# Linear attention's second pass: products of the features with the sums in row halves of the array, two heads each

## The chip, the cores and the metric

The kernel runs on one core of a Trainium2 chip. The metric is the device time of one execution in microseconds. Of the kernel before there are three runs (1293.9, 1294.66 and 1296.31 us; median 1294.66) and one profiled execution. Engines are named as in the profile: PE is the matmul engine (PEld its weight loads), DVE, ACT and POOL are the vector, scalar and general engines, SP issues the DMAs.

## The reference

Four layers are applied to x of 2048 tokens by 512, each as x + layer(layernorm(x)): A, B, A, B. The change lies in the A layers, linear attention with 32 heads of 16 columns:

```python
pq = jnp.einsum("bhsd,hdf->bhsf", q, w_phi)
pk = jnp.einsum("bhsd,hdf->bhsf", k, w_phi)
phi_q = jnp.concatenate([_softmax(pq, axis=-1), _softmax(-pq, axis=-1)], axis=-1)
phi_k = jnp.concatenate([_softmax(pk, axis=-1), _softmax(-pk, axis=-1)], axis=-1)
kv = jnp.einsum("bhsf,bhsd->bhfd", phi_k, v)
z  = jnp.einsum("bhsf->bhf", phi_k)
num = jnp.einsum("bhqf,bhfd->bhqd", phi_q, kv)
den = jnp.einsum("bhqf,bhf->bhq", phi_q, z)[..., None] + 1e-6
o = num / den
return (lambda x, *d: x.transpose(*d))(o, 0, 2, 1, 3).reshape(B, S, D) @ wo
```

A head has 32 features (two softmaxes of 16), so 4 heads fill 128 partitions. The B layers are causal softmax attention within four segments plus a memory over the segments before.

## The kernel before, in words

An A layer runs in two passes over 16 tiles of 128 tokens. `pass1` projects q, k and v, forms the features of k, and sums kv and z over all tokens into `kva`: 128 partitions (4 heads of 32 features), 8 groups g of 4 heads, 17 columns (16 of v and the ones column for z). At its end (L948 to L954) it builds `KN`, a block-diagonal copy of the sums: for each group 128 partitions by 4 heads x 17 = 68 columns, zero where the partition's head is not the column's. DVE does this with a 0/1 table (`bdA`, columns of the constant `bd`), four groups to an instruction.

`pass2` (L1017) then takes the tiles i = 0 to 15 one after the other. For each:

- `transposed` (L973) turns the features of q by PE into `f`, 128 features by 8 groups by 128 tokens. The transposes go in the two row halves of the array (64 tokens each, `tp_halves`, L183), into the banks mx and my (or lg), and ACT copies each half of the tokens to `f` (names P in the profile).
- `products` (L996) multiplies `f` with `KN`. For each group there are two matmuls in the two column halves of the array: 128 features by 64 tokens as weights, the 68 columns of `KN` moving, so that tokens 0 to 63 and 64 to 127 of four heads come out side by side in one bank. Features and sums are plain float32, and the trace records each matmul of that type twice (two passes, each with its own weight load). Most other matmuls are of a rounded type and recorded once.
- `weigh` (L551) divides by the ones column: a reciprocal and a multiplication on DVE, into the tile's output `o` (names U, later ot).
- `turn_halves` and `out_proj` turn `o` and multiply it with the output weight `wo` (names w; oh and ol are the halves of the turned tile). These matmuls fill all 128 rows and 128 columns.

PE's order is fixed: `held` (L165) ties every matmul to the one recorded before it. DVE, ACT, POOL and SP are held to their recorded order as well (`Ordered`, L145). PSUM has eight banks: four in rotation under the tag g, two under lg (taken together), mx and my.

For tiles 0 to 12 (`wide`) the products use both banks of lg, groups 0 to 3 in the first and 4 to 7 in the second, and one `weigh` takes both. The last three tiles run as side work in the opening of the B layer that follows (`steps`, L1494), between its first matmuls; lg is needed there, so each half of the groups takes one bank of g, and `weigh` takes it at once. `steps` hands out that side work over 11 slots by an estimate of PE time that `mm` (L174) adds up. The maxima of the B layer (`maxima`, L1256; CUSTOM_DVE_ANT_0 in the profile, ISA in the order of instructions) use banks mx, my and pairs of g in the same stretch.

In the profile all matmuls stand under L177, the transposes under L181 and L187, all operations of the other engines under L155.

Of the kernel before, what the change touches and what calls it, by code (L numbers as in the profile page):

```python
# [7 lines left out]
F32 = mybir.dt.float32  # L8
# [7 lines left out]
D = 512  # L16
H = 32
DH = 16
P = 128
# [3 lines left out]
VW = DH + 1  # L23
# [9 lines left out]
G = 4  # L33
# [68 lines left out]
def interleave_kernel(ctx, tc, x_in, a_wqkv, a_wphi, a_wo, b_wq, b_wk, b_wv, b_wo, b_beta,  # L102
                      c_ident, c_mask, c_bd, out):
    nc = tc.nc
    MUL, ADD, SUB, MAX, MIN = ALU.mult, ALU.add, ALU.subtract, ALU.max, ALU.min

    cp = ctx.enter_context(tc.tile_pool(name="cp", bufs=1))
    wp = ctx.enter_context(tc.tile_pool(name="wp", bufs=4))
    hp_ = ctx.enter_context(tc.tile_pool(name="hp", bufs=2))
    sp = ctx.enter_context(tc.tile_pool(name="sp", bufs=2))  # L110
# [5 lines left out]
    def nm(s):  # L116
        uid[0] += 1
        return f"{s}_{uid[0]}"
# [4 lines left out]
    def PS(tag, bufs, shape=(P, 512)):  # L123
        return ps.tile(list(shape), F32, tag=tag, bufs=bufs, name=nm(tag))
# [38 lines left out]
    dve, act, pool, sync = [Ordered(e) for e in (nc.vector, nc.scalar, nc.gpsimd, nc.sync)]  # L163
# [10 lines left out]
    def mm(*a, **k):  # L174
        n = a[0].free_size()
        work[0] += n / 2.26 if k["rhs"].dtype == F32R else (n * 2 / 2.4 + 25 if "tile_position" in k else 2 * max(112, n * 2 / 2.4))
        return held(nc.tensor.matmul(*a, **k))  # L177
# [13 lines left out]
        sync.dma_start(out=out.bitcast(F32), in_=in_.bitcast(F32))  # L191

    ident = cp.tile([P, P], F32, name="ident")
    bd = cp.tile([P, 27], F32, name="bd")
    bdA, bdB = bd[:, 0:8], bd[:, 8:16]
    mask = cp.tile([P, 512], F32, name="mask")
    gates = cp.tile([P, 2, H], F32, name="gates")
    eb = cp.tile([P, H], F32, name="eb")
# [3 lines left out]
    def constants():  # L202

        sync.dma_start(out=mask, in_=c_mask)
        sync.dma_start(out=eb, in_=b_beta.unsqueeze(0).broadcast_to([P, H]))
        yield
        yield
        act.activation(eb, eb, AF.Exp, scale=-1.0)
        dve.tensor_scalar(eb, eb, 1.0, None, op0=ADD)
        dve.reciprocal(gates[:, 1, :], eb)  # L210
        dve.tensor_scalar(gates[:, 0, :], gates[:, 1, :], -1.0, 1.0, op0=MUL, op1=ADD)
        for j in range(4):
            dve.tensor_copy(share[32 * j : 32 * j + 32, :].rearrange("p (c f) -> p c f", f=2),
                            gates[32 * j : 32 * j + 32, 0, :].rearrange("p (c j f) -> p j c f", j=4, f=2)[:, j])
        dve.tensor_scalar(share, share, -1.0, bd[:, 24:25], op0=ADD, op1=MUL)
        dve.tensor_scalar(share, share, 1.0, None, op0=ADD)
        dve.tensor_tensor(out=gates[:, 1, :].rearrange("p (c h) -> p c h", c=NC), op=MUL,
                          in0=gates[:, 1, :].rearrange("p (c h) -> p c h", c=NC),
                          in1=bdB.unsqueeze(1).broadcast_to([P, NC, 8]))
        dve.tensor_copy(ones, bd[0:32, 25:26].broadcast_to([32, P]))  # L220


    def wtiles(tag):
# [451 lines left out]
    class LayerA:  # L675
# [4 lines left out]
        def first(self, hT, vv, upcoming):  # L680
# [18 lines left out]

            for c in range(NC):  # L700
                pool.tensor_tensor(out=phibd[:, c], in0=wph[:, c, :].unsqueeze(1).broadcast_to([P, 8, DH]),
                                        in1=bd[:, 16:24].unsqueeze(2).broadcast_to([P, 8, DH]), op=MUL)
            kf, qf = [], []
            kfold, qfold = folded(kraw, kf), folded(qraw, qf)
            for t in range(4):
# [40 lines left out]
        def pass1(self, first):  # L746
# [44 lines left out]
            for n, s in enumerate(SEGS):  # L791
# [53 lines left out]
                if n < NSEG - 1:  # L845
                    hTs, g = upc
# [98 lines left out]
                self.e = {4 * s + i: e[4 + i] for i in range(3)}  # L945
                yield from self.transposed(0)
                yield from sums[1]
                KN = self.KN = sp.tile([P, 8, 4, VW], F32, tag="KN", bufs=1, name=nm("KN"))  # L948
                den = kva[:, :, DH]
                dve.tensor_scalar(den, den, 0.5e-6, None, op0=ADD)  # L950
                for g in (0, 4):
                    dve.tensor_tensor(out=KN[:, g : g + 4], op=MUL,
                                      in0=kva[:, g : g + 4, :].unsqueeze(2).broadcast_to([P, 4, 4, VW]),
                                      in1=bdA[:, 0:4].unsqueeze(1).unsqueeze(3).broadcast_to([P, 4, 4, VW]))  # L954
                exp(e[6])
                for j, _ in enumerate(qproj(3, e, later)):
                    if j == 1:
# [38 lines left out]
        def products(self, i):  # L996

            f, o = self.phT.pop(i), self.o
            wide = i <= NT - 4
            pns = PS("lg", 1, (P, 2, 512)) if wide else None  # L1000
            for half in range(2):
                pn = pns[:, half] if wide else PS("g", G)
                for q in range(4):
                    g = 4 * half + q
                    for a in (0, 64):
                        mm(pn[a : a + 64, q * 4 * VW : (q + 1) * 4 * VW], lhsT=f[:, g, a : a + 64],
                           rhs=self.KN[:, g].rearrange("p h e -> p (h e)"), start=True, stop=True,
                           tile_position=(0, a))
                if not wide:
                    weigh(o[:, half * 256 : half * 256 + 256].rearrange("p (g h d) -> p g h d", g=4, h=4),  # L1010
                          pn[:, 0 : 16 * VW].rearrange("p (g h e) -> p g h e", g=4, h=4), 0.0, False)
                elif half == 1:
                    weigh(o.rearrange("p (s h d) -> p s h d", s=2, h=16),
                          pns[:, :, 0 : 16 * VW].rearrange("p s (h e) -> p s h e", e=VW), 0.0, False)
                yield

        def pass2(self):  # L1017
# [686 lines left out]
```

## Time and profile before

| | |
|---|---|
| median of three runs | 1294.66 us |
| profiled execution | 1295.97 us, its span 1294.2 us |
| busy PE, PEld, DVE, ACT, POOL | 1257.7, 975.4, 1070.7, 838.5, 754.0 us |
| granted PE clock | 1.0 |
| KN built, first and second A layer | 171.8 and 803.4 us |
| first and last product of all | 173.3 and 904.5 us |

Busy shares are means over the whole span. Matmuls are pipelined: a matmul's row shows its full length from first weight to last result, so that neighbours overlap, and what one costs is read from the distance between starts. "128*64 128x68" in a row means weights of 128 rows by 64 columns and a moving part of 128 rows by 68 columns.

### The profile page before, as it was taken

Reading aid. Unit: us, or ns where it says so; the run is one execution under the profiler, and the core shown is the slowest. Engines: PE = TensorE matmul, PEld = TensorE weight load, DVE = VectorE, ACT = ScalarE, POOL = GpSimd, SP = SyncE. Lnnn points to the kernel's source line nnn. Section 1 sums busy time; section 2 is a strip of 40 time slices with the busy share of each in tenths; the row PEclk is TensorE's granted clock in tenths of the full one; section 3 lists DMA queues with packets and bytes.
Section 4 is the critical chain, followed back from the end, with each engine's and each line's share of the span. In section 5 each row is a group of like instructions: output and inputs, shape, how many; then the busy total and the mean of one; then the engine's idle time right before and its main releaser. Section 6 shows DMA issues by size and latency. Waiting matters only on the chain.

```text
span 1294.2 us, 42658 instructions
## 1 busy us (share of the span) xinstructions
PE 1257.7 (97%) x16832; PEld 975.4 (75%) x16832; DVE 1070.7 (83%) x3471; ACT 838.5 (65%) x1256; POOL 754.0 (58%) x1122
## 2 busy tenths in 40 slices
PE   8999999999999999999999999999999999999987
PEld 7887877777777777777668887777777777778765
DVE  5776878689898998998767768887899899898995
ACT  6556446557787787686644434554778867877754
POOL 1668856225667667667324347662457666767653
PEclk9999999999999999999999999999999999999999
DMA  6397358545565555555351102856456545544432
GB/s 215 107 352 259 110 194 262 171 116 151 168 183 149 146 136 149 148 139 169 110 186 42 66 34 84 278 170 174 140 144 200 156 136 145 145 140 117 117 84 83
DMA packets 134423, 196.64 MB, mean 152 GB/s; under 512 B 15440, under 2 KB 61648, under 8 KB 133456
## 3 DMA queue, kind: packets, MB, share of 16 engines
q1 hardware_dynamic: 133408, 193.80, 49.3%
q8 instruction: 134, 2.20, 0.7%
q14 instruction: 65, 0.53, 0.1%
q10 hardware_dynamic: 816, 0.11, 0.1%
HBM read 101.05 MB, written 39.85 MB: 109 GB/s over the span
## 4 chain that ended last, share of the span: by engine, by line
PE 76%; DVE 13%; ACT 3%; POOL 3%; issue 3%; DMA 2%; SPq 1%; DVEq 0%; POOLq 0%; ACTq 0%
PE g L177 60%; PE lg L177 7%; PE mx L177 4%; PE g L181 3%; DVE g L155 2%; ACT P L155 2%; DVE U L155 2%; DVE mx L155 1%; PE my L177 1%; POOL P L155 1%; DVE my L155 1%; DVE es L155 1%; DVE mxs L155 1%; DVE bs L155 1%; DVE ol L155 1%
## 5 line engine op out<-in xcount | busy, mean ns | idle before, releaser
L155 ACT ACTIVATE P<-lg 128x1024 f32<-128x1024 f32 x316 | 324.4, 1026 | 96.3 <-PE lg L177 77.0
L155 POOL TENSOR_SCALAR_AFFINE_SELECT P<-P 128x256 f32<-128x256 f32 (+1 forms) x448 | 189.9, 441 | 231.1 <-ACT P L155 212.3
L155 DVE CUSTOM_DVE_ANT_0 g<-g,mask 128x128 f32<-128x128 f32 (+3 forms) x392 | 189.7, 539 | 7.4 <-PE g L177 6.9
L155 DVE CUSTOM_DVE_ANT_0 mx<-mx,mask 128x512 f32<-128x512 f32 (+2 forms) x316 | 159.4, 504 | 40.6 <-PE my L177 31.2
L177 PE MATMUL g<-hh,wqk 64*128 64x512 f32 (+1 forms) x960 | 184.4, 392 | 0.9 <-SPq L155 0.6
L177 PE MATMUL g<-w,oh 64*128 64x512 f32 (+2 forms) x848 | 160.9, 380 | 3.9 <-ACT oh L155 2.6
L155 DVE CUSTOM_DVE_ANT_0 my<-my,mask 128x512 f32<-128x512 f32 (+2 forms) x316 | 164.4, 520 | 0.0
L177 PE MATMUL lg<-e,e 64*128 64x512 f32 (+1 forms) x1010 | 146.4, 343 | 7.5 <-ACT P L155 7.5
L177 PE MATMUL g<-P,v 128*32 128x128 f32 (+3 forms) x2064 | 151.6, 433 | 0.2
L155 DVE DVE_READ_ACCUMULATOR2_ANT mxs<- 128x1 f32 x1024 | 145.8, 142 | 0.0
L177 PE MATMUL g<-w,hh 64*128 64x512 f32 (+1 forms) x672 | 141.3, 394 | 0.8 <-SPq L155 0.4
L177 PEld LDWEIGHTS lg<-e,e 64*128 64x128 f32 x1010 | 93.3, 184 | 51.9 <-ACT P L155 19.6
L177 PEld LDWEIGHTS g<-hh,wqk 64*128 64x128 f32 (+1 forms) x960 | 102.3, 185 | 17.9 <-SPq L155 1.2
L177 PEld LDWEIGHTS g<-P,v 128*32 128x32 f32 x2064 | 64.9, 109 | 61.4 <-issue 53.4
L177 PEld LDWEIGHTS g<-w,oh 64*128 64x128 f32 (+1 forms) x848 | 94.6, 186 | 21.8 <-ACT oh L155 3.5
L155 ACT COPY tb<-g 128x512 f32<-128x512 f32 (+1 forms) x132 | 71.2, 576 | 53.6 <-PE g L177 53.3
L177 PE MATMUL g<-hl,wqk 64*128 64x512 f32 (+1 forms) x480 | 103.6, 389 | 0.0
L177 PE MATMUL g<-w,ol 64*128 64x512 f32 (+2 forms) x424 | 100.2, 378 | 1.8 <-DVE ol L155 1.6
L177 PEld LDWEIGHTS g<-w,hh 64*128 64x128 f32 (+1 forms) x672 | 82.3, 186 | 16.8 <-SPq L155 1.1
L177 PE MATMUL g<-w,hl 64*128 64x512 f32 (+1 forms) x336 | 87.8, 390 | 0.0
L155 ACT ACTIVATE P<-P 128x1024 f32<-128x1024 f32 x64 | 68.1, 1069 | 28.8 <-POOL P L155 28.5
L155 POOL TENSOR_TENSOR ta<-tb,ta 128x512 fp32r<-128x512 f32 x60 | 76.3, 1291 | 14.2 <-ACT ta L155 11.2
(174 smaller groups left out, 2957.5 us busy)
## 6 DMA issues: line engine op xcount, KB each, us to landing
e<-ta SPq DMA_DIRECT2D x384, 128.0 KB
wqk<-wqk SPq DMA_DIRECT2D x128, 256.0 KB
x<-x SPq DMA_DIRECT2D x48, 256.0 KB
pq<-tb SPq DMA_DIRECT2D x24, 256.0 KB
tb<-pq SPq DMA_DIRECT2D x24, 256.0 KB
x<-xr SPq DMA_DIRECT2D x22, 256.0 KB
xr<-x SPq DMA_DIRECT2D x20, 256.0 KB
x<-in SPq DMA_DIRECT2D x16, 256.0 KB
```

Source lines behind the costliest of these rows:

```text
L155: i = f(*a, **k)
L177: return held(nc.tensor.matmul(*a, **k))
L181: return held(nc.tensor.transpose(*a))
```

## The change

Each group of four heads is cut into two pairs of heads. Heads 0 and 1 of a group fill partitions 0 to 63 of `f`, heads 2 and 3 partitions 64 to 127. A matmul now has 64 features by all 128 tokens as weights and the 34 columns of its two heads moving; the two matmuls of a group run in the row halves of the array, the first into one bank, the second into another. There are as many matmuls as before.

What follows from it: `KN` has 34 columns for a group, from a table of two columns, and is built in one instruction. A tile's output has the heads in another order (the first pairs of all groups, then the second pairs), and the rows of the output weight are handed over in this order; they are permuted on the host. The wide `weigh` takes the two banks as before. For the last three tiles both banks of g are taken at the start and both are weighed after the second half of the groups. The columns of the constant `bd` move, and it has 21 instead of 27.

```diff
-    bd = cp.tile([P, 27], F32, name="bd")
-    bdA, bdB = bd[:, 0:8], bd[:, 8:16]
+    bd = cp.tile([P, 21], F32, name="bd")
+    bdA, bdB = bd[:, 19:21], bd[:, 0:8]
...
-                KN = self.KN = sp.tile([P, 8, 4, VW], F32, tag="KN", bufs=1, name=nm("KN"))
+                KN = self.KN = sp.tile([P, 8, 2, VW], F32, tag="KN", bufs=1, name=nm("KN"))
                 den = kva[:, :, DH]
                 dve.tensor_scalar(den, den, 0.5e-6, None, op0=ADD)
-                for g in (0, 4):
-                    dve.tensor_tensor(out=KN[:, g : g + 4], op=MUL,
-                                      in0=kva[:, g : g + 4, :].unsqueeze(2).broadcast_to([P, 4, 4, VW]),
-                                      in1=bdA[:, 0:4].unsqueeze(1).unsqueeze(3).broadcast_to([P, 4, 4, VW]))
+                dve.tensor_tensor(out=KN, in0=kva.unsqueeze(2).broadcast_to([P, 8, 2, VW]), op=MUL,
+                                  in1=bdA.unsqueeze(1).unsqueeze(3).broadcast_to([P, 8, 2, VW]))
...
-            pns = PS("lg", 1, (P, 2, 512)) if wide else None
+            if wide:
+                both = PS("lg", 1, (P, 2, 512))
+                pns = [both[:, r] for r in range(2)]
+            else:
+                pns = [PS("g", G) for _ in range(2)]
             for half in range(2):
-                pn = pns[:, half] if wide else PS("g", G)
-                for q in range(4):
-                    g = 4 * half + q
-                    for a in (0, 64):
-                        mm(pn[a : a + 64, q * 4 * VW : (q + 1) * 4 * VW], lhsT=f[:, g, a : a + 64],
-                           rhs=self.KN[:, g].rearrange("p h e -> p (h e)"), start=True, stop=True,
-                           tile_position=(0, a))
-                if not wide:
-                    weigh(o[:, half * 256 : half * 256 + 256].rearrange("p (g h d) -> p g h d", g=4, h=4),
-                          pn[:, 0 : 16 * VW].rearrange("p (g h e) -> p g h e", g=4, h=4), 0.0, False)
+                for g in range(4 * half, 4 * half + 4):
+                    for r, pn in enumerate(pns):
+                        mm(pn[:, g * 2 * VW : (g + 1) * 2 * VW], lhsT=f[64 * r : 64 * r + 64, g, :],
+                           rhs=self.KN[64 * r : 64 * r + 64, g].rearrange("p h e -> p (h e)"),
+                           start=True, stop=True, tile_position=(64 * r, 0))
+                if half == 1 and wide:
+                    weigh(o.rearrange("p (s h d) -> p s h d", s=2, h=16),
+                          both[:, :, 0 : 16 * VW].rearrange("p s (h e) -> p s h e", e=VW), 0.0, False)
                 elif half == 1:
-                    weigh(o.rearrange("p (s h d) -> p s h d", s=2, h=16),
-                          pns[:, :, 0 : 16 * VW].rearrange("p s (h e) -> p s h e", e=VW), 0.0, False)
+                    for r, pn in enumerate(pns):
+                        weigh(o[:, r * 256 : r * 256 + 256].rearrange("p (g h d) -> p g h d", g=4, h=4),
+                              pn[:, 0 : 16 * VW].rearrange("p (g h e) -> p g h e", g=4, h=4), 0.0, False)
                 yield
...
-    bd[p, p // 32] = 1.0
+    bd[p, 19 + p // 32 % 2] = 1.0
...
+    wo = np.asarray(A_wo).reshape(8, 2, 2 * DH, D).transpose(1, 0, 2, 3).reshape(D, D)
```

On PE almost every instruction keeps its place, and the products change in form alone. The order changes where the last three tiles run. First DVE at tile 13 of the first A layer. The rows are the maxima (each ISA row with a bank is followed by the reading of its accumulator, mxs) and the weighing (RECIPROCAL and TENSOR_TENSOR into ot). Before:

```order
L155 ISA my_3766,mxs_2827<-my_3766,mask 128x384
L155 ISA mxs_2827 128x1
L155 RECIPROCAL r_3794<-g_3785 128x16
L155 TENSOR_TENSOR ot_3740<-g_3785,r_3794 128x256
L155 ISA g_3797,mxs_2827<-g_3797,mask 128x256
L155 ISA mxs_2827 128x1
L155 ISA g_3798,mxs_2827<-g_3798,mask 128x256
L155 ISA mxs_2827 128x1
L155 ISA g_3797,mxs_2827<-g_3797,mask 128x256
L155 ISA mxs_2827 128x1
L155 ISA g_3798,mxs_2827<-g_3798,mask 128x256
L155 ISA mxs_2827 128x1
```

And now, from the second of the four maxima on:

```order
L155 ISA g_3795,mxs_2826<-g_3795,mask 128x256
L155 ISA mxs_2826 128x1
L155 ISA g_3794,mxs_2826<-g_3794,mask 128x256
L155 ISA mxs_2826 128x1
L155 ISA g_3795,mxs_2826<-g_3795,mask 128x256
L155 ISA mxs_2826 128x1
L155 RECIPROCAL r_3812<-g_3784 128x16
L155 TENSOR_TENSOR ot_3739<-g_3784,r_3812 128x256
L155 RECIPROCAL r_3815<-g_3785 128x16
L155 TENSOR_TENSOR ot_3739<-g_3785,r_3815 128x256
L155 ISA mx_3829,mxs_2826<-mx_3829,mask 128x512
```

The weighing of the first bank stood ahead of the four maxima on g; both weighings now stand behind them, next to each other.

Then PE at the same place, from the second half of tile 13's products to those of tile 14 (g<-KN,P), with the transposes of tile 15 (lg<-ident,P) and a pair of maxima (mx, my) between. Before:

```order
L177 MATMUL g_3807<-KN_2297,P_550_3448 64x68 x8
L177 MATMUL mx_3819<-e_433_2831,e_432_2830 128x512
L177 MATMUL my_3820<-e_433_2831,e_432_2830 128x512
L187 MATMUL lg_3827<-ident,P_541_3406 128x64 x16
L177 MATMUL g_3845<-KN_2297,P_602_3741 64x68 x8
L177 MATMUL g_3857<-KN_2297,P_602_3741 64x68 x8
```

And now:

```order
L177 MATMUL g_3784<-KN_2297,P_550_3447 128x34
L177 MATMUL g_3785<-KN_2297,P_550_3447 128x34
L187 MATMUL lg_3820<-ident,P_541_3405 128x64 x8
L177 MATMUL mx_3829<-e_433_2830,e_432_2829 128x512
L177 MATMUL my_3830<-e_433_2830,e_432_2829 128x512
L187 MATMUL lg_3820<-ident,P_541_3405 128x64 x8
L177 MATMUL g_3844<-KN_2297,P_602_3740 128x34
L177 MATMUL g_3845<-KN_2297,P_602_3740 128x34
```

Half of the transposes moved one slot earlier, ahead of the pair of maxima, and the products alternate between the two banks. The second A layer has the same differences.

More of the change, by code (lines that the diff above doesn't have):

```diff
@@ L214, in constants @@
                             gates[32 * j : 32 * j + 32, 0, :].rearrange("p (c j f) -> p j c f", j=4, f=2)[:, j])
-        dve.tensor_scalar(share, share, -1.0, bd[:, 24:25], op0=ADD, op1=MUL)
+        dve.tensor_scalar(share, share, -1.0, bd[:, 16:17], op0=ADD, op1=MUL)
         dve.tensor_scalar(share, share, 1.0, None, op0=ADD)
@@ L219, in constants @@
                           in1=bdB.unsqueeze(1).broadcast_to([P, NC, 8]))
-        dve.tensor_copy(ones, bd[0:32, 25:26].broadcast_to([32, P]))
+        dve.tensor_copy(ones, bd[0:32, 17:18].broadcast_to([32, P]))
     def wtiles(tag):
@@ L701, in first @@
                 pool.tensor_tensor(out=phibd[:, c], in0=wph[:, c, :].unsqueeze(1).broadcast_to([P, 8, DH]),
-                                        in1=bd[:, 16:24].unsqueeze(2).broadcast_to([P, 8, DH]), op=MUL)
+                                        in1=bd[:, 8:16].unsqueeze(2).broadcast_to([P, 8, DH]), op=MUL)
             kf, qf = [], []
@@ L1682 @@
     p = np.arange(P)
-    bd = np.zeros((P, 27), np.float32)
-    bd[[16, 33, 80, 97], 26] = 0.5e-6
-    bd[[15, 31], 25] = -1.0
-    bd[p, 24] = p % 32 < 16
-    bd[p, 16 + p // 16] = 1.0
-    bd[p, p // 32] = 1.0
+    bd = np.zeros((P, 21), np.float32)
+    bd[[16, 33, 80, 97], 18] = 0.5e-6
+    bd[[15, 31], 17] = -1.0
+    bd[p, 16] = p % 32 < 16
+    bd[p, 8 + p // 16] = 1.0
+    bd[p, 19 + p // 32 % 2] = 1.0
     hb = (p % 2) * 4 + p // 32 % 2 * 2 + p // 64
-    bd[p, 8 + hb] = 1.0
-    ins = [np.ascontiguousarray(np.asarray(A_x)[0]), A_wqkv, A_w_phi, A_wo, B_wq, B_wk, B_wv, B_wo, B_beta,
+    bd[p, hb] = 1.0
+    wo = np.asarray(A_wo).reshape(8, 2, 2 * DH, D).transpose(1, 0, 2, 3).reshape(D, D)
+    ins = [np.ascontiguousarray(np.asarray(A_x)[0]), A_wqkv, A_w_phi, wo, B_wq, B_wk, B_wv, B_wo, B_beta,
            ident, mask, bd]
```

## The prediction

> **What bounds the kernel now.** I read the page first (busy shares, chain of waits), then the groups of instructions with shapes kept apart, the tiles' own views, and last the timeline around the products.
>
> ```profile
> PE 1257.7 (97%) x16832; PEld 975.4 (75%) x16832; DVE 1070.7 (83%) x3471; ACT 838.5 (65%) x1256; POOL 754.0 (58%) x1122
> PE 76%; DVE 13%; ACT 3%; POOL 3%; issue 3%; DMA 2%; SPq 1%; DVEq 0%; POOLq 0%; ACTq 0%
> ```
>
> TensorE is busy for 97% of the span and carries 76% of the chain that ended last, so a longer or shorter stretch of PE goes to the end unless PE waits for somebody soon after. What the change touches on PE are the products with the sums (output lg or g, inputs KN and P). In the groups (count | busy, mean ns of one) they stand beside the forms that I need to price the new one:
>
> ```profile
> L177 PE MATMUL g<-KN,P 128*64 128x68 f32 x192 | 7.6, 228 | 0.0
> L177 PEld LDWEIGHTS lg<-KN,P 128*64 128x64 f32 x832 | 27.4, 137 | 7.4 <-ACT P L155 6.0
> L177 PEld LDWEIGHTS lg<-e,e 64*128 64x128 f32 x1010 | 93.3, 184 | 51.9 <-ACT P L155 19.6 <-issue 13.4 <-ACT ta L155 4.1
> L177 PEld LDWEIGHTS mx<-phibd,e 128*128 128x128 f32 x16 | 1.9, 192 | 0.0
> L187 PEld LDWEIGHTS mx<-ident,P 64*128 64x128 f32 x192 | 13.8, 139 | 2.8 <-POOL P L155 1.2 <-issue 1.1 <-DVE KN L155 0.4
> ```
>
> A product's load of 64 columns takes 137 ns, a load of 128 columns 184 or 192, whether it fills 64 rows (e,e, in the rounded type) or 128 (phibd, plain float32 as the products are). Only the transposes load 128 columns in 139 ns. How much of a load is really time on the array is seen where it is not hidden. A tile's view gives shortest, median and longest duration:
>
> ```profile
> L177 PE MATMUL lg<-KN,P x832: 222/223/274, 173.3 to 871.4; 128*64 128x68 f32 x167
> L187 PE MATMUL mx<-ident,P x192: 222/222/272, 172.7 to 862.3; 64*128 64x64 f32 x192
> L177 PE MATMUL g<-hh,wqk x960: 383/391/501, 241.3 to 1218.5; 64*128 64x512 f32 x178, 128*128 128x512 f32 x14
> ```
>
> With the 192 passes above there are 1024: 32 tiles (16 in each of two linear layers) of 16 matmuls, every one recorded twice. The longest ones are firsts of a run, whose load nothing covers: a 64-column load shows as 51 ns, a transpose's 128-column load as 50, an ordinary 128-column load as 110.
>
> Now one tile on PE: last transpose, products, first matmul of the output projection (start, length).
>
> ```profile
> 199.06 0.22 PE L187 MATMUL mx<-ident,P 64*128 64x64 f32 x1
> 199.50 0.22 PE L187 MATMUL my<-ident,P 64*128 64x64 f32 x1
> 199.66 1.17 PE L177 MATMUL lg<-KN,P 128*64 128x68 f32 x32
> 200.75 0.73 PE L177 MATMUL g<-w,oh 128*128 128x512 f32 x2
> ```
>
> From the last transpose to the projection it is 1.25 us: 0.15 to change over, 32 passes of which the last starts 1.17 - 0.22 = 0.95 later, 0.15 to change over again. Two passes run side by side in the column halves, so a pair takes 0.95 / 16 = 0.059 us. That covers a 64-column load (0.05); load and 68 moving columns are about equally long.
>
> **The change, part by part.** *The products.* A tile still has 32 passes in 16 pairs, but each has half the moving columns (34) and twice the weight columns (128, over 64 rows). The trace has no plain float32 matmul of 64*128 other than transposes. The bounds for one pair: from below the transposes in the same halves, 8 pairs from 199.06 to 199.50, so 0.063. From above the following rows; first PE and PEld in the halves, then the full array:
>
> ```profile
> 294.55 0.28 PE L177 MATMUL mx<-e,e 63*128 63x256 f32 x1
> 294.56 0.28 PE L177 MATMUL my<-e,e 63*128 63x256 f32 x1
> 294.67 0.27 PE L177 MATMUL mx<-e,e 63*128 63x256 f32 x1
> 294.55 0.19 PEld L177 LDWEIGHTS mx<-e,e 63*128 63x128 f32 x1
> 294.56 0.19 PEld L177 LDWEIGHTS my<-e,e 63*128 63x128 f32 x1
> 30.24 1.06 PE L177 MATMUL mx<-phibd,e 128*128 128x128 f32 x8
> 31.13 1.06 PE L177 MATMUL my<-phibd,e 128*128 128x128 f32 x8
> ```
>
> The two halves load together (294.55 and 294.56) and the next pair comes 0.12 later, so two 128-column loads side by side cost one, not two. In the full array plain float32 passes with 128-column loads come every (31.13 - 30.24) / 8 = 0.111. The moving part is no longer than the load in either row, so the load alone explains the pace. I take 0.115, between the two rows nearest in load, and not the transposes' 0.063, because their loads are the only short ones (139 ns against 192). The halved moving columns then bring nothing: they end up under a load that has doubled.
>
> [...]
>
> A regular tile becomes 16 x 0.115 + 0.15 = 1.99 us against 1.25: +0.74. The 0.15 at the front goes, since transposes and products now have the same form; the 0.15 behind stays. Eleven tiles of a layer (0, 1, 4 to 12) are regular. Tiles 2 and 3 wait for the features' copies:
>
> ```profile
> 181.33 0.46 PE L187 MATMUL g<-ident,U 64*128 64x64 f32 x8
> 182.22 0.33 PE L177 MATMUL lg<-KN,P 128*64 128x68 f32 x2 [0.42 <-ACT P L155]
> 182.71 1.16 PE L177 MATMUL lg<-KN,P 128*64 128x68 f32 x30 [0.15 <-ACT P L155]
> 183.80 0.50 PE L177 MATMUL g<-w,oh 128*128 128x512 f32 x1
> ```
>
> The first half of the tokens could start at 182.22; now every matmul needs both copies, so all starts at 182.71, with an open load: 0.11 + 15 x 0.115 + 0.15 = 1.98 against 183.80 - 182.71 = 1.09, +0.89 each.
>
> *The last three tiles* run in the next layer's opening, on g banks, of which there are four:
>
> ```profile
> 269.03 0.69 PE L177 MATMUL g<-KN,P 128*64 128x68 f32 x16
> 269.65 0.50 PE L177 MATMUL g<-e,e 63*128 63x256 f32 x4
> 270.38 0.25 DVE L155 RECIPROCAL r<-g 128x16 f32<-128x16 f32 x1
> 271.01 0.42 DVE L155 CUSTOM_DVE_ANT_0 g<-g,mask 128x256 f32<-128x256 f32 x1
> 271.63 2.42 PE L177 MATMUL g<-KN,P 128*64 128x68 f32 x64
> 272.50 0.25 DVE L155 RECIPROCAL r<-g 128x16 f32<-128x16 f32 x1
> 273.13 0.69 DVE L155 CUSTOM_DVE_ANT_0 mx<-mx,mask 128x512 f32<-128x512 f32 x1
> 273.98 0.50 PE L177 MATMUL lg<-e,e 64*128 64x512 f32 x2
> ```
>
> Tile 13: each half of 8 pairs took 0.62 (269.03 to 269.65) and takes 0.92, less some 0.15 for changeovers and an open load that go: +0.3 for both. Tiles 14 and 15: 271.63 to 273.98 is 2.35; 32 pairs make 3.68, less 0.14: +1.2. Here the change also adds a wait. Tile 13 takes two banks at once and DVE empties both behind the four maxima, where it emptied the first ahead of them (270.38). By DVE's rows the four take 272.50 - 271.01 = 1.5 and a weighing 273.13 - 272.50 = 0.63; starting at 270.4, when DVE comes free of the maxima ahead of them, both banks are free at about 270.4 + 1.5 + 2 x 0.65 = 273.2. Tile 14 takes over these banks and PE is there at 271.63 + 0.3 = 271.9, so PE and all that stands behind it wait 1.3 us. It lies between 0 (if DVE gets to the maxima sooner) and 1.5 (if they wait for PE too).
>
> Sum for a layer: 11 x 0.74 + 2 x 0.89 + 0.3 + 1.2 + 1.3 = 12.7 us; two layers, 25.4.
>
> *What PE's present waits take back.* In the pass PE waits for others; behind such a wait a slower product costs nothing:
>
> ```profile
> 215.73 0.74 PE L177 MATMUL g<-w,oh 128*128 128x512 f32 x2
> 216.91 0.50 PE L177 MATMUL g<-w,ol 128*128 128x512 f32 x1 [0.45 <-DVE ol L155]
> 232.10 1.17 PE L177 MATMUL lg<-KN,P 128*64 128x68 f32 x32
> 233.79 0.70 PE L177 MATMUL g<-w,oh 128*128 128x512 f32 x2 [0.52 <-DVE ot L155]
> 234.96 0.50 PE L177 MATMUL g<-w,ol 128*128 128x512 f32 x1 [0.46 <-DVE ol L155]
> ```
>
> Tile 1's +0.74 goes into tile 2's wait (PE is free at 181.7 and starts in earnest at 182.71). By the starts, 216.91 is 0.6 later than PE alone would be, and 233.79 and 234.96 another 0.6 each; these are set by DVE. With tile 1 that is 2.5 to 2.8 a layer, 5.5 in both. It may be 0, if those DVE chains slip along with PE, or more, if all of PE's waits of the pass swallow. Their sum is bounded by the first row below, PE's busy time from 172 to 265: 93 less 89.06 is 3.9 us, and as the tail of the matmul ahead of a wait counts as busy (0.2 for each of some seven), 5.3 a layer, 10.6 in both.
>
> ```profile
> 172.00:265.00 93.00, 89.06 (x981) 1.00 0.65 202
> L155 DVE TENSOR_TENSOR KN<-kva,bd x4: 429/438/1184, 171.8 to 803.4; 128x272 f32<-128x272 f32 x4
> ```
>
> *At no cost.* KN is built in one DVE instruction instead of two, 0.4 us less for each layer (second row). It is hidden: from 171.8 two of them end at about 172.7, and the first products come at 173.3, behind transposes. The weighing has the same elements. The constants' columns and the order of the output weight's rows change no instruction's size.
>
> Forecast: 25.4 - 5.5 = +19.9 on the profiled execution's 1295.97 us, 1315.9. That execution lay 1.3 above the median of the three runs, 1294.66, so 1314.6 for the median, rounded to 1315.
>
> **Rivals.**
>
> *A, faster: short columns decide.* If the new loads run at the transposes' price (139 ns, 0.063 a pair) and the last tiles' banks are free in time, a regular tile takes 16 x 0.063 + 0.15 = 1.16, 0.09 less than 1.25, and the last three tiles together 0.8 less; tiles 2 and 3 stay. That is 1.7 us a layer, 3.5 in both, of which PE's waits give back some 0.5: 1292 for the median. It decides from below 0.069 a pair, where 16 pairs and one changeover equal 1.25. For it: same halves, same 64*128 form. Against it: every load of 128 columns that is no transpose takes 184 to 192 ns. [...]
>
> *B, no measurable change: cheap loads, but the banks take the gain.* With 0.063 a pair PE comes to tile 14 at about 271.4 and still finds its banks taken until 273.2; 32 pairs then end at about 275.1 instead of 273.98, 1.1 us later, which eats the 1.2 us that the other tiles of a layer gain: 1294. What speaks against A's loads speaks against it too. Nor can waits hide the forecast's cost: 10.6 of 25.4 at most.
>
> *C, much slower: the halves load in turn*, 0.22 a pair. Each pair costs 0.105 more than forecast, 32 x 16 pairs 54 us: 1369. The rows at 294.55 and 294.56 speak against it.
>
> **How the numbers follow.** The forecast has 0.87, A 0.07, B 0.05, C 0.01. Its range goes from a pair at 0.107 (just under the open load's 0.11) with no new wait and all of PE's waits swallowing (9.4 us a layer, 18.7 less 10.6: 1303) to 0.12 with the new wait at 1.5 and nothing swallowed (14.2 a layer: 1323). About 0.2%, 2.6 us, can be told from no change. Chances: faster 0.07, same 0.05, slower 0.88.
>
> **What would show it.** Right: LDWEIGHTS of KN,P at 184 to 192 ns, 32 passes from first to last start in about 1.75 us, no changeover gap ahead of them, each regular tile longer by 0.7, a PE wait for DVE ahead of the products of tile 14, and busy PE up by some 20 us. Wrong: loads at 139 ns, or a pair below 0.07.

## The result and the profile after

The changed kernel takes 1318.91 us (median of 4 runs, 1316.54 to 1321.42), the kernel before 1295.36 us beside it: a ratio of 1.0183, 95% interval 1.0169 to 1.0196, 23.6 us slower. The profiled execution is the slowest of the four, 1321.42 us with a span of 1319.7, 25.5 above that of before. So direction and size came as forecast (1315, range 1303 to 1323). The trace shows that the sum behind it did not: about half of the loss comes from something that no step of it has, so part of the match is luck.

The changed kernel's page, busy times, granted clock by slices, and the chain of waits:

```profile
PE 1285.3 (97%) x16832; PEld 1010.5 (77%) x16832; DVE 1070.2 (81%) x3469; ACT 837.5 (63%) x1256; POOL 753.8 (57%) x1122
PEclk9999999989999999999999999898899999999999
PE 82%; DVE 12%; ACT 2%; issue 1%; DMA 1%; POOL 1%; SPq 0%; DVEq 0%; POOLq 0%; ACTq 0%
```

TensorE has as many instructions as before and is busy 27.6 us longer. In the row of the granted clock there are four slices with an 8; before it was 1.00 over the whole span. That is the part which the prediction doesn't have.

First what it does have. The products in the changed kernel's tile view (count, shortest, median and longest duration, first and last start):

```profile
L177 PEld LDWEIGHTS lg<-KN,P x832: 182/188/333, 173.5 to 892.3; 64*128 64x128 f32 x167
L177 PE MATMUL lg<-KN,P x832: 247/274/404, 173.6 to 892.4; 64*128 64x34 f32 x167
```

The load now takes 188 ns instead of 137, as the phibd and e,e loads did (192 and 184), and not the transposes' 139. The matmul shows as 274 ns against 223 before, although it moves half as many columns: it is longer by 51 ns, as its load is. The longest ones (333 and 404 ns) belong to the stretches at a lower clock.

The changed kernel's timeline, one regular tile (last transpose, products, projection) and then the place of tiles 13 to 15:

```profile
203.05 0.22 PE L187 MATMUL my<-ident,P 64*128 64x64 f32 x1
203.12 1.93 PE L177 MATMUL lg<-KN,P 64*128 64x34 f32 x32
204.97 0.51 PE L177 MATMUL g<-w,oh 128*128 128x512 f32 x1
...
280.22 0.46 DVE L155 CUSTOM_DVE_ANT_0 g<-g,mask 128x256 f32<-128x256 f32 x1
280.44 0.66 PE L177 MATMUL g<-KN,P 64*128 64x34 f32 x4
280.60 0.25 DVE L155 RECIPROCAL r<-g 128x16 f32<-128x16 f32 x1
280.88 0.42 DVE L155 TENSOR_TENSOR ot<-g,r 128x256 f32<-128x256 f32 x1
281.51 0.42 DVE L155 TENSOR_TENSOR ot<-g,r 128x256 f32<-128x256 f32 x1
283.67 0.84 PE L177 MATMUL g<-KN,P 64*128 64x34 f32 x6
```

In the regular tile the products follow the last transpose after 0.06 us, one transposed pair's time: the gap at the front is gone. The last of the 32 starts 1.65 us after the first (1.93 - 0.27, but for the rounding of the row), over 15 steps 0.110 a pair, and the projection comes 0.20 behind it. From transpose to projection it is 1.92 us against 1.25, +0.67.

At tile 14 the products begin at 280.44, while DVE reads the fourth maximum and before it weighs tile 13 (280.60 to 281.93). So tile 14 does not wait for tile 13's banks. Its first four products (the row shows no more of them) take 0.66 us where 0.27 + 0.11 would do: 0.28 of pause at most, not 1.3. The last row is three pairs at 283.67: (0.84 - 0.40) / 2 = 0.22 apart, twice as far as in the regular tile.

That is the clock. The changed kernel's windows (stretch, its length, busy time of PE, PEld, DVE, ACT and POOL, then the granted clock, DMA share and GB/s). The first three follow each other, the others are all further stretches below full clock before the end:

```profile
279.91:283.32 3.41, 3.41 (x64) 3.25 (x60) 3.34 (x15) 1.01 (x1) 0.00 (x0) 1.00 0.90 203
283.32:286.73 3.41, 3.41 (x29) 2.99 (x26) 2.52 (x11) 0.55 (x1) 0.00 (x0) 0.50 0.04 9
286.73:290.15 3.42, 3.42 (x8) 2.69 (x9) 2.03 (x12) 0.47 (x1) 0.41 (x1) 0.50 0.00 0
170.68:174.09 3.41, 3.41 (x28) 2.46 (x26) 0.61 (x2) 0.60 (x2) 0.00 (x0) 0.50 0.02 5
249.18:252.59 3.41, 3.41 (x9) 2.63 (x8) 0.43 (x1) 0.00 (x0) 0.00 (x0) 0.50 0.62 208
832.86:839.69 6.83, 6.83 (x41) 5.75 (x40) 3.94 (x6) 2.24 (x4) 4.23 (x5) 0.50 0.77 282
890.89:897.72 6.83, 6.83 (x32) 5.70 (x31) 1.05 (x2) 0.00 (x0) 0.00 (x0) 0.50 0.54 176
928.44:935.27 6.83, 6.83 (x35) 5.64 (x34) 4.51 (x19) 1.02 (x1) 0.41 (x1) 0.50 0.01 3
```

Six times TensorE runs at half clock, for 3.41 or 6.83 us, 34 us in all. Five of them begin in or right behind products, the one at 170.68 ahead of the first one (173.6), so that products can't have brought it. In order of time all starts lie on one grid: they are 23, 10, 161, 17 and 11 times 3.413 us apart (from 170.68 to 928.44 it is 757.76 us, 222 such steps). In the first row, the window ahead of a drop, PE is never idle; it starts some 60 matmuls, most of them products. That holds for the window ahead of 928.44 too, but not for the other four (last section). The second window (x29) begins with products too and is followed by another at half clock; that third one holds eight long matmuls, and full clock is back behind it.

Where the 25.5 us arise is read by cutting the span where the products begin and end in each layer (first product, then the e,e matmul behind the last). The windows of before, and then of the changed kernel (one profiled execution of each):

```profile
0.00:173.32 173.32, 166.55 (x1786) 137.08 (x1786) 119.70 (x210) 94.58 (x171) 107.17 (x134) 1.00 0.60 207
173.32:273.98 100.66, 96.72 (x1114) 75.11 (x1111) 80.87 (x200) 54.35 (x97) 49.43 (x60) 1.00 0.65 200
273.98:803.86 529.88, 523.23 (x7230) 402.87 (x7227) 448.22 (x1522) 350.76 (x494) 308.74 (x473) 1.00 0.43 127
803.86:904.69 100.83, 96.74 (x1114) 75.09 (x1110) 80.64 (x200) 54.63 (x98) 49.46 (x60) 1.00 0.68 212
904.69:1294.20 389.51, 374.49 (x5603) 285.29 (x5600) 341.29 (x1341) 284.22 (x397) 239.23 (x395) 1.00 0.47 134
```

```profile
0.00:173.55 173.55, 165.97 (x1786) 137.73 (x1788) 118.82 (x209) 94.30 (x171) 107.15 (x134) 0.99 0.60 206
173.55:285.37 111.82, 108.91 (x1117) 89.47 (x1115) 83.19 (x206) 54.33 (x97) 49.37 (x60) 0.97 0.60 181
285.37:814.65 529.28, 522.51 (x7227) 404.78 (x7228) 446.10 (x1515) 350.52 (x494) 308.69 (x473) 1.00 0.44 127
814.65:930.60 115.95, 113.29 (x1119) 93.21 (x1117) 83.26 (x207) 54.53 (x98) 49.37 (x60) 0.93 0.61 185
930.60:1319.70 389.10, 374.61 (x5600) 285.27 (x5598) 338.86 (x1334) 283.80 (x397) 239.22 (x395) 0.99 0.47 133
```

Stretch by stretch the change costs +0.2, +11.2, -0.6, +15.1 and -0.4 us. The two passes have the same work, but one costs 4 us more than the other; theirs are also the lowest clocks, 0.97 and 0.93.

### The profile page after: what moved, and what is told of

Its sections match the earlier page's. It is cut to its first block, busy times and chain, and to the rows that moved or that the text cites. A ratio compares the mean times of both kernels' runs of the same rounds, so it can differ in the third digit from the quotient of the medians.

```text
span 1319.7 us, 42650 instructions
## 1 busy us (share of the span) xinstructions
PE 1285.3 (97%) x16832; PEld 1010.5 (77%) x16832; DVE 1070.2 (81%) x3469; ACT 837.5 (63%) x1256; POOL 753.8 (57%) x1122
## 4 chain that ended last, share of the span: by engine, by line
PE 82%; DVE 12%; ACT 2%; issue 1%; DMA 1%; POOL 1%; SPq 0%; DVEq 0%; POOLq 0%; ACTq 0%
PE g L177 63%; PE lg L177 9%; PE mx L177 3%; PE g L181 3%; DVE g L155 2%; DVE U L155 2%; PE my L177 2%; DVE mx L155 1%; DVE my L155 1%; ACT P L155 1%; DVE mxs L155 1%; PE mx L187 1%; DVE es L155 1%; DVE wt L155 0%; DVE r L155 0%
## 5 line engine op out<-in xcount | busy, mean ns | idle before, releaser
L177 PE MATMUL g<-w,hh 64*128 64x512 f32 (+1 forms) x672 | 144.2, 397 | 0.3 <-issue 0.2
L155 DVE DVE_READ_ACCUMULATOR2_ANT mxs<- 128x1 f32 x1024 | 141.8, 139 | 0.0
L177 PEld LDWEIGHTS g<-w,hh 64*128 64x128 f32 (+1 forms) x672 | 84.8, 189 | 15.1 <-PE my L177 0.7
L177 PE MATMUL mx<-e,e 63*128 63x256 f32 (+3 forms) x323 | 82.6, 320 | 0.9 <-DMA e<-ta 0.6
```

Of the source, the lines that this page charges most:

```text
L155: i = f(*a, **k)
```

## The experiments

Two theories were to be told apart. One, the prediction's: the load of 128 weight columns sets the pace of a pair, and moving columns under it are free. The other: TensorE waits (for banks, for copies), or the pace has another cause. After the first runs the clock was added as a second cause beside the load. All kernels were run in rounds with the kernel before. The first four shared one chip (before 1294.78 us), the next four another (before 1295.16), the last two a third (before 1296.74). Where an edit alters all products, the planner's estimate of their time was kept at that of the kernel which it starts from, so that the order of the work stays.

### The changed kernel again

> The changed kernel once more, on the same chip as the next three. Both theories: about 1319 us (1316 to 1322), products 0.110 us a pair, and some stretches of 3.4 or 6.8 us at half the granted clock near the products. Should the clock stay at 1.0 throughout, the half-clock stretches are no property of the change and the time should be about 1306 (1318.9 less some 14 us that these stretches cost in the profile).

1315.55 us (1312.69 to 1316.23), ratio 1.0152 (1.0136 to 1.0169), +20.8 us, just under the range expected. In its profiled execution a pair again takes 0.110, but there are 17 us at half clock instead of 34, and that execution is 5.2 us shorter than the first one's. Its first pass, from first product to the e,e matmul behind the last, runs at full clock throughout:

```profile
173.02:282.06 109.04, 106.09 (x1117) 87.08 (x1115) 82.95 (x206) 54.35 (x97) 49.38 (x60) 1.00 0.62 186
```

That is +8.4 us against the 100.66 of before: what the change costs in a pass without the half clock.

### 64 moving columns instead of 34

The 30 columns more are never read.

```diff
-                        mm(pn[:, g * 2 * VW : (g + 1) * 2 * VW], lhsT=f[64 * r : 64 * r + 64, g, :],
-                           rhs=self.KN[64 * r : 64 * r + 64, g].rearrange("p h e -> p (h e)"),
+                        mm(pn[:, g * 64 : (g + 1) * 64], lhsT=f[64 * r : 64 * r + 64, g, :],
+                           rhs=self.KNF[64 * r : 64 * r + 64, g * 2 * VW : g * 2 * VW + 64],
```

> As the changed kernel, but every product moves 64 columns instead of 34 (the 30 further ones are never read). [...] Theory that the half clock comes from too little moving work: the granted clock goes to 1.0 and the time falls by about 14 us to about 1305 (1302 to 1310), although the work grows. Rival, that the half clock has another cause (waits, chance): clock about 0.99 and 1319 us. Rival, that moving columns set the pace: a pair at 0.13 us or more and some 1328 us.

1310.87 us (1308.56 to 1312.49), ratio 1.0119 (1.0102 to 1.0136). A regular tile's products on its timeline:

```profile
201.94 1.95 PE L177 MATMUL lg<-KN,P 64*128 64x64 f32 x32
```

(1.95 - 0.27) / 15 = 0.112 a pair, against 0.110 with 34: nearly twice the moving columns cost next to nothing a pair. But the kernel is 4.7 us faster than the changed one beside it, with more work. Its runs have clocks of 0.997 and 0.998, those of the changed kernel 0.990 to 0.993. So the theory of too little moving work has the direction right, but not the size: it expected a clock of 1.0, some 14 us less and 1302 to 1310.

### Loads of 64 columns, in quarters of the array

The changed kernel, with each matmul cut into two halves of the tokens.

```diff
-                        mm(pn[:, g * 2 * VW : (g + 1) * 2 * VW], lhsT=f[64 * r : 64 * r + 64, g, :],
-                           rhs=self.KN[64 * r : 64 * r + 64, g].rearrange("p h e -> p (h e)"),
-                           start=True, stop=True, tile_position=(64 * r, 0))
+                        for t in (0, 64):
+                            mm(pn[t : t + 64, g * 2 * VW : (g + 1) * 2 * VW], lhsT=f[64 * r : 64 * r + 64, g, t : t + 64],
+                               rhs=self.KN[64 * r : 64 * r + 64, g].rearrange("p h e -> p (h e)"),
+                               start=True, stop=True, tile_position=(64 * r, t))
```

> As the changed kernel (row halves, two banks, 34 columns, output in the new order), but each matmul is cut into two column halves of 64 tokens, so that a load has 64 columns again and four matmuls run side by side. Load theory: four of them take about 0.06 us, loads at 137 ns, a tile's products last 0.95 us from first to last start as before the change, clock 1.0, and the time is back at 1294 to 1299 us. Rival, that the row form, the two banks or the later weighing cost the time: 1305 us or more.

1295.32 us (1293.31 to 1301.49, 10 runs), ratio 1.0005 (0.9992 to 1.0018): the whole loss is gone. Its loads and a tile's products, from its tile view and its timeline:

```profile
L177 PEld LDWEIGHTS lg<-KN,P x1664: 129/135/228, 172.5 to 877.0; 64*64 64x64 f32 x185
```

```profile
204.19 1.14 PE L177 MATMUL lg<-KN,P 64*64 64x34 f32 x64
```

Twice as many passes take 1.14 us instead of 1.93: four start together every (1.14 - 0.22) / 15 = 0.061. All else of the change (the order of heads, one KN, two banks at once for the last tiles) is still in, so what costs is the load of 128 columns (188 ns in the changed kernel, 135 here with 64). The clock does not stay at the 1.0 expected (0.994 to 0.999): two of the ten runs take some 6 us more (1300.98 and 1301.49), and the profiled one, 1301.49, has 10.24 us at half clock, from 805.55 on, at the second layer's first tiles. The version does not beat the kernel before: with half the moving columns its mean step of 0.061 is hardly shorter than the 0.063 of before, so the load of 64 columns seems to set it.

### One matmul over the whole array

The kernel before, with the two column halves made one matmul of 128 rows, 128 weight columns and 68 moving ones.

```diff
-                    for a in (0, 64):
-                        mm(pn[a : a + 64, q * 4 * VW : (q + 1) * 4 * VW], lhsT=f[:, g, a : a + 64],
-                           rhs=self.KN[:, g].rearrange("p h e -> p (h e)"), start=True, stop=True,
-                           tile_position=(0, a))
+                    mm(pn[:, q * 4 * VW : (q + 1) * 4 * VW], lhsT=f[:, g, :],
+                       rhs=self.KN[:, g].rearrange("p h e -> p (h e)"), start=True, stop=True)
```

> The kernel before, but with one matmul for each group of four heads over the whole array: 128 features, 128 tokens, 68 moving columns. Load theory: a pass takes one 128-column load, 0.110 us, so that a tile's 16 passes last 1.65 us, as long as the 16 pairs of the row halves. With 57 of 110 ns moving the clock theory has the clock at 1.0 and about 1305 us (1302 to 1310); without it 1319. Rival, that the halves hinder each other: a pass below 0.08 us and about 1300 us or less.

1314.02 us (1311.83 to 1317.92), ratio 1.0148 (1.0126 to 1.0171).

```profile
203.10 2.00 PE L177 MATMUL lg<-KN,P 128*128 128x68 f32 x16
```

(2.00 - 0.28) / 15 = 0.115 a matmul, though the order of heads and the banks are those of before. The cost comes with the 128 columns, not with the row halves; and two halves that load side by side (0.110 a pair) cost no more than one load over all rows. The time lies between the two that were expected, 1302 to 1310 and 1319; the clocks are 0.996 to 1.000, and the profiled execution has two stretches of 3.41 us at half clock.

### Only the last three tiles in row halves

> The kernel before, with the last three tiles of each linear layer alone in row halves (34 columns, two banks taken at once, weighed behind the maxima). Load theory with the wait of 0.25 us for a bank that the changed kernel's trace shows: in that trace the stretch from the first products of tile 13 to the first matmul behind tile 15 grew from 4.95 to 6.65 us, so 3.4 us for both layers: 1298 (1296 to 1301), more by up to 6 us where half-clock stretches follow these tiles. The forecast's own terms (0.3 + 1.2 + 1.3 a layer) would give 5.6 more: 1300.4.

```diff
+                            mm(pn[:, g * 2 * VW : (g + 1) * 2 * VW], lhsT=f[64 * r : 64 * r + 64, g, :],
+                               rhs=self.KN[64 * r : 64 * r + 64, g, 2 * r : 2 * r + 2].rearrange("p h e -> p (h e)"),
+                               start=True, stop=True, tile_position=(64 * r, 0))
```

1302.88 us (1298.81 to 1305.03), ratio 1.0052 (1.0032 to 1.0072), +7.7, clocks of 0.995 and 0.996. This kernel's windows behind those tiles, one in each layer:

```profile
276.08:282.91 6.83, 6.83 (x24) 5.10 (x22) 3.80 (x17) 1.02 (x1) 0.41 (x1) 0.50 0.00 0
910.96:917.79 6.83, 6.83 (x40) 5.85 (x39) 4.99 (x22) 1.02 (x1) 0.41 (x1) 0.50 0.06 14
```

Three tiles alone bring TensorE down to half clock, behind them in both layers and nowhere else before the end. 6.83 us at half clock lose up to 3.4, twice 6.8; the products themselves should cost some 3.

### The change without them

The changed kernel, with the last three tiles in quarters of the array.

```diff
+                        for t, n in ((0, P),) if wide else ((0, 64), (64, 64)):
+                            mm(pn[t : t + n, g * 2 * VW : (g + 1) * 2 * VW], lhsT=f[64 * r : 64 * r + 64, g, t : t + n],
+                               rhs=self.KN[64 * r : 64 * r + 64, g].rearrange("p h e -> p (h e)"),
+                               start=True, stop=True, tile_position=(64 * r, t))
```

> The changed kernel, with the last three tiles of each layer cut into column halves of 64 tokens as well, so that their loads have 64 columns; tiles 0 to 12 stay in row halves. Load theory: 26 tiles of some 0.67 us more are 17 us, of which PE's waits take 5: 1307, and 2 to 6 us more for half-clock stretches behind the first tiles. Its rise and that of the run with the last tiles alone add up to that of the changed kernel (20 us on this chip). Rival, that the last tiles carry most of the cost: 1300 or less.

1317.61 us (1313.08 to 1323.52), ratio 1.0172 (1.0139 to 1.0205), +22.5: a miss. This part should have cost less than the whole change and costs as much. The clocks of its four runs are 0.988 to 0.997, and the profiled one (1323.52) has 24 us at half clock, 17 of them in one piece at the second layer's first tiles. So the parts do not add up (7.7 + 22.5 against 20.8 or 23.6), and a split of the loss by tiles can't be had in this way: the half clock strikes at other places when something moves.

### 17 moving columns

The changed kernel, which leaves out the second head of each pair: 17 columns move, and the output repeats the first head's.

```diff
-                           rhs=self.KN[64 * r : 64 * r + 64, g].rearrange("p h e -> p (h e)"),
+                           rhs=self.KN[64 * r : 64 * r + 64, g, 0],
```

> As the changed kernel, but every product moves only the 17 columns of one head; the sums' columns of the second head of each pair are left out, and its output repeats the first head's. Load theory: a pair stays at 0.110 us, so nothing is gained from half the moving work. Clock theory (half clock where too little moves for too long): more half-clock stretches than with 34 columns, clock below 0.990, and the time goes up by 2 to 8 us, to about 1320, although PE has less to do. Rival without the clock theory: 1314 to 1316, clock as with 34 columns. Rival that moving columns set the pace: a pair at 0.08 us or less and 1305 or less.

1325.96 us (1319.69 to 1329.33), ratio 1.0228 (1.0194 to 1.0263): with half the moving work the slowest kernel of all, by more than the 2 to 8 us expected (+30.8 us against before, the change +20.8 to +23.6 in its three rounds).

```profile
200.95 1.91 PE L177 MATMUL lg<-KN,P 64*128 64x17 f32 x32
```

(1.91 - 0.26) / 15 = 0.110 a pair, the same. The clocks are the lowest: 0.979 to 0.988.

### The whole array with 120 moving columns

The matmul over the whole array from above; 52 columns more are never read.

```diff
-                    mm(pn[:, q * 4 * VW : (q + 1) * 4 * VW], lhsT=f[:, g, :],
-                       rhs=self.KN[:, g].rearrange("p h e -> p (h e)"), start=True, stop=True)
+                    mm(pn[:, q * P : q * P + 120], lhsT=f[:, g, :],
+                       rhs=self.KNF[:, g * 4 * VW : g * 4 * VW + 120], start=True, stop=True)
```

> As the run over the whole array, but every product moves 120 columns instead of 68 (the 52 further ones are never read). [...] Clock theory: clock 1.0 in all runs and a time of 1308 to 1313, which is then the price of the loads alone. Rival: time up by 5 us or more against 68 columns.

1311.57 us (1311.11 to 1314.02), ratio 1.0128 (1.0112 to 1.0145), clocks 0.999 and 1.000. Its two passes, from first product to the e,e matmul behind the last:

```profile
174.06:283.90 109.84, 106.89 (x860) 87.03 (x856) 83.72 (x207) 54.38 (x97) 49.42 (x60) 1.00 0.62 184
812.10:922.22 110.12, 106.88 (x859) 87.04 (x855) 83.70 (x207) 54.70 (x98) 49.44 (x60) 1.00 0.64 194
```

The passes cost +9.2 and +9.3 us, alike in both layers, at full clock.

A tile's products on its timeline, (2.04 - 0.28) / 15 = 0.117 a matmul:

```profile
203.52 2.04 PE L177 MATMUL lg<-KN,P 128*128 128x120 f32 x16
```

### The change itself with 100 moving columns

The changed kernel; what the 66 more columns write is written over by the next group or never read.

```diff
-                        mm(pn[:, g * 2 * VW : (g + 1) * 2 * VW], lhsT=f[64 * r : 64 * r + 64, g, :],
-                           rhs=self.KN[64 * r : 64 * r + 64, g].rearrange("p h e -> p (h e)"),
+                        mm(pn[:, g * 2 * VW : g * 2 * VW + 100], lhsT=f[64 * r : 64 * r + 64, g, :],
+                           rhs=self.KNF[64 * r : 64 * r + 64, g * 2 * VW : g * 2 * VW + 100],
```

> The changed kernel, with 100 moving columns in each product instead of 34; the 66 more are written over by the next group or never read, and the order of all instructions stays. Theory (the load sets the pace of a pair; what is lost beyond that is lost to stretches at half clock, which follow a stretch of 3.41 us with little moving work): a pair stays at 0.11 us, since 100 columns move in about 0.083 us; the array is moving 75% of each pair's time instead of 25%, so no stretch at half clock, a clock of 0.998 or more, and a time 14 to 17 us above the kernel before, so 2 to 10 us below the changed kernel on the same chip, though TensorE is given three times the columns. Rival 1 (the stretches come from something else that the change brings, its waits or its loads): the stretches stay, clock 0.986 to 0.993, and the time is that of the changed kernel or more. Rival 2 (moving columns count after all): a pair at 0.13 or more, 10 us above the changed kernel.

And the changed kernel beside it:

> The changed kernel as it is, beside the one with 100 moving columns on the same chip. All theories: 17 to 26 us above the kernel before, clock 0.986 to 0.993, stretches at half clock of 3.41 or 6.83 us round the products.

With 100 columns 1307.82 us (1306.13 to 1308.78, 6 runs), ratio 1.0080 (1.0067 to 1.0093), clock 0.999 to 1.000 in all runs. The changed kernel beside it takes 1317.86 us (1313.85 to 1323.77, 5 runs), ratio 1.0159 (1.0136 to 1.0181), clock 0.986 to 0.995. Three times the columns save 10.0 us, while a pair takes a little longer on the mean of a tile, (1.98 - 0.27) / 15 = 0.114:

```profile
201.84 1.98 PE L177 MATMUL lg<-KN,P 64*128 64x100 f32 x32
```

The single starts show that only the first step is longer (0.142 us against 0.084 with 34 columns); from there on a pair takes 0.112 in both, and so does a matmul over the whole array with 68 or 120 columns.

Order, waits, loads and banks are those of the changed kernel, so it is the wider moving work that keeps the clock full, and not a change in one of them. The kernel with 100 columns, cut like the two above:

```profile
0.00:172.34 172.34, 163.54 (x1786) 135.80 (x1788) 118.78 (x209) 94.28 (x171) 107.29 (x135) 1.00 0.60 208
172.34:281.89 109.55, 106.71 (x1118) 87.09 (x1115) 83.11 (x205) 54.34 (x97) 49.44 (x60) 1.00 0.62 185
281.89:808.38 526.49, 519.89 (x7230) 404.16 (x7227) 446.78 (x1516) 350.35 (x494) 308.45 (x474) 1.00 0.44 128
808.38:918.16 109.78, 106.79 (x1114) 87.14 (x1113) 83.12 (x205) 54.56 (x98) 49.45 (x60) 1.00 0.64 194
918.16:1304.90 386.74, 372.59 (x5602) 287.14 (x5600) 339.35 (x1336) 283.76 (x397) 239.20 (x395) 1.00 0.48 134
```

Against before: -1.0, +8.9, -3.4, +9.0 and -2.8, together +10.7. Against this, the changed kernel's profiled execution loses another 1.2, 2.3, 2.8, 6.2 and 2.4, together 14.8, to 34 us at half clock. The loads alone were expected to cost 14 to 17 us and cost 11, since the stretches outside the passes are 7.2 us shorter than before.

## Why the prediction was right, and where it was not

**The price of a pair** is right. The load of 128 columns sets it: 0.110 measured, 0.115 taken. 17, 34, 64 and 100 moving columns change the mean by 4% at most, by the first step alone, and loads of 64 bring it back to 0.061. No run shows the 0.107 at the lower end of the range: the lowest mean was 0.110. Nor does one show what moving columns take by themselves, 57 ns for 68 and 0.083 us for 100 in two of the expectations: with 68 a step took 0.059 us in the kernel before, and a pair with 100 took 0.114. (For the kernel before, the prediction divided 0.95 by 16, though 16 pairs have 15 steps. The single starts give 0.11 for the first, open load and 0.059 from there on, so the number stands.) Rival A (short columns decide, loads at the transposes' price) falls, and B with it; C (halves load in turn) too, since a pair in halves costs no more than one load in the whole array.

**The regular tile** came out at +0.67 instead of +0.74: the pair was 0.005 too dear, the gap at the front is 0.06 where one load (0.115) was counted, and the gap behind is 0.20 instead of 0.15.

**The new wait at tile 14** is the term of the sum that failed, 1.3 us a layer. The step was "Tile 14 takes over these banks", tile 13's. The timeline shows tile 14 at work before tile 13 is weighed, so it has other banks. They are those of the maxima: its first loads for the one bank and for the other start at 280.41 and 280.79, right behind the third and the fourth maximum (read by 280.36 and 280.74). 0.28 us at most is left of the wait.

**PE's waits in the pass.** Without that bank term the sum is 11.4 us a layer, less 2.75 for waits, 8.7. The passes at full clock cost 8.9 and 9.0 with 100 columns. There a pair takes 0.114, nearly the 0.115 of the forecast, and this part holds to 0.3 us; the changed kernel's own pass at full clock, in its second profile, cost 8.4. The rows show PE's idle time in a pass falling by 1.1 us (from 3.94 to 2.84 and from 4.09 to 2.99); that the rest of the 2.75 lies in waits that count as busy was argued, and is not shown.

**The stretches outside the passes** had no term. With 100 columns at full clock they are shorter than before by 1.0 us ahead of the first products, 3.4 behind the first pass and 2.8 behind the second, 7.2 in all. These are not waits that went: by the rows of the windows PE is idle there for 29.6 us against 28.4, and busy for 8.2 us less with nearly the same number of instructions. With 120 columns over the whole array, also at full clock, the same stretches are 0.7 longer, 1.7 and 2.0 shorter, 3.0 in all. Each figure is a single execution against a single one of before. So how much of it belongs to the change, and by what steps, stays open.

**The clock** had no term either: every duration was carried over as if TensorE's clock stayed at 1.00, as it did in the trace of before. Keeping it there is worth 10.0 us on the median (100 columns against 34 on one chip).

In the profiled executions it adds up so: of the +19.9 the passes brought 17.9 (the 2.0 less is about the bank wait), the stretches outside them took 7.2, and what lies between the profiles with 100 and with 34 columns, which is somewhat under half of the 34 us at half clock, added 14.8: +25.5. By its own mechanism alone, at full clock, the change would have cost some +11, as it does with 100 columns; that the forecast of +20 came out right is luck, since a cause that it didn't know made up for the bank wait that didn't come and for the shorter stretches. The changed kernel's runs in three rounds (+20.8, +21.1 and +23.6 us) are load plus clock. Of its marks, loads at 188 ns, first to last start in 1.65 us (1.75 forecast), no gap at the front and regular tiles longer by 0.7 were met; the PE wait ahead of tile 14 was not, and busy PE rose by 27.6 instead of 20, since it counts the half clock too (with 100 columns it rose by 11.8).

## What to carry to other kernels

Trading column halves for row halves gave each matmul twice the weight columns to load, and the row of a load went from 137 to 188 ns. Here, with 17 to 100 moving columns against 128 weight columns in plain float32, the load was the price (0.110 to 0.114 us a pair), and halving the moving work bought nothing. Before counting on a shorter matmul, compare the pace of the two forms in the trace, load against moving columns, and see which of the two sets it. And look at the granted clock after a change that makes TensorE's work thinner: this kernel, 97% busy, ran at half clock for 34 us, and even padding the moving side from 34 to 100 columns (0.114 a pair instead of 0.110) paid against the changed kernel, by 10.0 us, though not against the kernel before.

## What the hardware showed that was not expected

TensorE's clock fell to half in a kernel whose PE is busy for 97% of the span. How often it fell goes with how much of a pair's time the columns move. The pace below is the mean step within a tile. The share is an estimate: the number of moving columns by 0.87 ns (0.059 us for 68 columns, the steps behind the first in the kernel before) over the pace. It is an upper one, since 34 columns in quarters go at nearly that step too. Clocks are those of all runs of a kernel.

| products | pace, us | moving share | granted clock |
|---|---|---|---|
| before, 68 columns | 0.063 | 0.94 | 0.998 to 1.000 |
| whole array, 120 | 0.117 | 0.89 | 0.999 to 1.000 |
| row halves, 100 | 0.114 | 0.76 | 0.999 to 1.000 |
| whole array, 68 | 0.115 | 0.51 | 0.996 to 1.000 |
| row halves, 64 | 0.112 | 0.50 | 0.997 to 0.998 |
| quarters, 34 | 0.061 | 0.48 | 0.994 to 0.999 |
| row halves, 34 (the change, 13 runs) | 0.110 | 0.27 | 0.986 to 0.995 |
| row halves, 17 | 0.110 | 0.13 | 0.979 to 0.988 |

Thin moving work is not all of it. Ahead of four of the six drops in the changed kernel's first profile PE has pauses: it is busy for 1.80, 2.68, 2.45 and 2.30 us of the 3.41 ahead of 170.68, 249.18, 832.86 and 890.89, and for all of it ahead of 283.32 and 928.44. Pauses alone don't do it either. The first row is the window ahead of 832.86; the second is the kernel with 100 columns at the same tile, a stretch as long, with the same busy time and the same wait for the features' copies, and no drop behind it:

```profile
829.45:832.86 3.41, 2.45 (x48) 2.07 (x48) 1.64 (x4) 2.36 (x5) 1.42 (x2) 1.00 0.93 303
823.88:827.30 3.42, 2.45 (x54) 2.31 (x52) 1.24 (x3) 2.58 (x5) 1.86 (x3) 1.00 0.94 312
```

So pauses and thin work seem to count together. What brings the drop at 170.68 is not shown: no product lies in the window ahead of it, but a pause of 1.61 us and other matmuls of 17 columns. The profile of the changed kernel beside the one with 100 columns has such a drop too, at 172.22, and stays at half clock for 17 us, into the first tiles. The traces of before and of the kernel with 100 columns have none there (granted clock 1.00 up to their first products at 173.32 and 172.34).

Ahead of the end, the stretches at half clock in these traces are one, two, three or five times 3.41 us long, and in the changed kernel's first profile all of them start on one grid of 3.413 us. Where it lies differs from run to run (drops at 283.32 in one profiled execution of the changed kernel, at 282.91 in another), and with it, if the clock goes by such stretches, what falls into one of them. On one chip the runs of the changed kernel spread over 9.9 us, those with 100 columns over 2.7. Idle time is not needed for a drop: in the stretch from 279.91 to 283.32, ahead of one, PE was busy for 3.41 of 3.41 us. In the table, clocks of 0.995 and less stand at shares of 0.27 and below and, in two runs of ten, at 0.48; from 0.76 on none is under 0.998. Whether there is a limit between 0.27 and 0.76, and how gaps within 3.41 us weigh against thin work, no run shows.
